# Feature maps of q for the last two batches: one projection and a crossbar transpose in place of a second projection

## The chip, the cores and the metric

The kernel runs on one core of one Trainium2 chip. The metric is the device time of one launch in microseconds. The core has TensorE (PE, with its weight loads PEld), VectorE (DVE), ScalarE (ACT), GpSimd (POOL, which here issues the loads) and SyncE (SP, which here issues transposes and stores).

## The reference

Linear attention with a softmax-like feature map, then a two-layer FFN with a squared ReLU. Eight batches of eight heads, 576 tokens, 64 columns a head; 128 features; the FFN goes from 512 over 2048 to 512.

```python
def phi(x):
    proj = np.einsum('bhsd,df->bhsf', x, w_phi)
    proj = proj - np.max(np.abs(proj), axis=-1, keepdims=True)
    return np.concatenate([np.exp(proj), np.exp(-proj)], axis=-1)
q_p, k_p = phi(q), phi(k)
kv  = np.einsum('bhsf,bhsd->bhfd', k_p, v);  z = np.sum(k_p, axis=2)
num = np.einsum('bhsf,bhfd->bhsd', q_p, kv)
den = np.einsum('bhsf,bhf->bhs', q_p, z)[..., None] + 1e-06
x = (num / den).transpose(0, 2, 1, 3).reshape(B * S, H * D)
h = np.maximum(x @ w_in, 0.0);  out = (h * h) @ w_out
```

## The kernel before

The attention of a batch and the FFN of a chunk of 512 tokens are interleaved: nine FFN chunks, the first 512 tokens of each batch as chunks 0 to 7, and the remaining 64 of all batches as chunk 8. The kernel first writes down some 1731 steps (`plan.add`), each with an engine, what it reads and writes, and the PSUM banks that it opens and closes. Then `arrange` puts them into the order of the table ORDER, with the bank of each from BASES and the choice between two engines from STATES. Every engine runs its own steps in that order and waits for what a step reads from others, so the table alone decides what stands behind what on each queue.

Of a batch (`attention`), in order of the steps' names:

- `Xk`, `Xq`: SP transposes the loaded, token-major xk and xq by DMA (18 blocks of 128x128) into kT and qT; xk, xq, kT and qT have two buffers, used by even and odd batches.
- `Pk`, `Mk`, `Ekp`, `Ekn`: projection of k (L354), its maximum (L409) and two exponentials (L415), token-major. `em`, `V`, `KV`, `kvc`: v is scaled by the maxima (L442), then kv is summed on PE (L472, L477) and copied to SBUF as bf16.
- The q side goes in five chunks c, four of 128 tokens by eight heads in half batches, and a last one of 64 tokens. `Pq` projects q token-major (L354) and `Mq` takes the maximum on DVE (L514); its exponential `en` scales the output later. `Fq` projects the same q a second time, feature-major (L549, two matmuls of 512 columns, of 256 for c = 4), and `Eqp`, `Eqn` take the exponentials on ACT (L564) into qp and qn.
- `NA`, `SA`, `NB`, `rd`, `xo`: numerators with qp (L579), scaled by `en` on DVE (L591), numerators with qn added, the reciprocal of the denominator (L599) and the product (L603). `Xx`: SP transposes xo into xT or xS (L637), the input of the FFN.

The FFN has `F1` (L719, four matmuls of 512 columns), `relu` (L694 on ACT or L696 on DVE), `sq` (L703), `F2` (L784), the copy `ot` (L195, L197) and the store `st` (L803).

Of the kernel before, what the change touches and what calls it, by code (L numbers as in the profile page):

```python
# [7 lines left out]
F32 = mybir.dt.float32  # L8
# [3 lines left out]
ACT = mybir.ActivationFunctionType  # L12
# [12 lines left out]
def dve_cost(n):  # L25
    return n / 960 + 0.064, n / 960 + 0.150 + SEM
# [85 lines left out]
def kernel(  # L112
# [41 lines left out]
    def sb(name, shape, dt=BF16):  # L154
        return pool.tile([P, *shape], dt, name=name)

    def ring(name, n, shape, dt=BF16):
        return [sb(f"{name}{i}", shape, dt) for i in range(n)]
# [19 lines left out]
    qp, qn = ring("qp", NQP, [8 * P]), ring("qn", NQP, [8 * P])  # L178
# [4 lines left out]
    mkn = sb("mkn", [36], F32)  # L183
# [132 lines left out]
    def attention(b):  # L316
# [181 lines left out]

        def qmax_ops(c):
# [17 lines left out]
            add("DVE", dve_cost(2 * n * Fd), fn, r=[pj], w=[("mq", s2, c)], closes=pj, what="Mq")  # L517
# [13 lines left out]

        qfeat = {}
# [128 lines left out]
        else:  # L661
# [17 lines left out]
            kv_ops(3)  # L679
            for c in range(5):  # L680
                qmax_ops(c)
            for c in range(5):
                q_ops(c)
                out_ops(c)
# [320 lines left out]
```

## Time and profile before

| what | before |
|---|---|
| median of 3 runs | 355.43 us (354.84 to 355.82) |
| span of the profiled execution (its own time is not listed) | 353.0 us |
| mean granted TensorE clock | 1.000 |
| PE, DVE, ACT, POOL busy | 340.7, 276.1, 226.8, 96.6 us |
| feature-major projections (L549) | 80 matmuls, 14.9 us busy |
| DMA transposes kT and qT; xT and xS | 6 and 6; 28 and 7 |

Busy times are unions of overlapping instructions: PE's matmuls are pipelined, and one of 512 columns lasts 379 ns in the table of groups while the next starts after 216 or so. What PE is waited for or waits for is therefore read from the chain of waits and not from the busy share. Batch 6's q side lies between about 210 and 257 us of the profile, batch 7's between about 235 and 286; after 300 us only FFN work is left.

### The profile page before, as it was taken

The numbers are of one execution on the slowest core, as the hardware profiler recorded it, in microseconds if no ns is written. First come the engines' busy times: TensorE is split into PE (matmuls) and PEld (weight loads), VectorE is DVE, ScalarE is ACT, GpSimd is POOL, SyncE is SP. The second block draws the span as 40 slices with busy tenths as digits, with TensorE's granted clock in tenths as the row PEclk, the third lists the DMA queues.
The fourth block names the chain that finished last, engine by engine and source line by source line (L and its number), as shares of the span: only waits on it lengthen the run. The fifth ranks groups of instructions, "written<-read, shape, count | busy, mean of one in ns | idle before, by whom it ended". The sixth has DMA issues, their size and how long they took to land.

```text
span 353.0 us, 8396 instructions
## 1 busy us (share of the span) xinstructions
PE 340.7 (97%) x3367; PEld 192.2 (54%) x3400; DVE 276.1 (78%) x524; ACT 226.8 (64%) x428; POOL 96.6 (27%) x144
## 2 busy tenths in 40 slices
PE   8889999999999999999999999999999999999995
PEld 5679875544654554545445654455555544444452
DVE  4999998899979988989678888799988727736210
ACT  4999887499688875785678577869676211340301
POOL 8745350488429300297001820000000000000000
PEclk9999999999999999999999999999999999999999
DMA  9999999899989976899354995600211211010105
GB/s 102 177 200 202 196 107 155 134 142 175 182 169 150 155 141 155 160 111 158 79 129 84 120 187 111 146 20 21 53 40 53 47 51 48 30 59 2 59 3 176
DMA packets 96101, 39.59 MB, mean 112 GB/s; under 512 B 64576, under 2 KB 91584, under 8 KB 96064
## 3 DMA queue, kind: packets, MB, share of 16 engines
q0 software_dynamic: 45216, 18.36, 45.6%
q1 hardware_dynamic: 50528, 20.42, 26.5%
q8 instruction: 26, 0.43, 0.5%
q10 hardware_dynamic: 320, 0.30, 0.3%
q14 instruction: 11, 0.09, 0.1%
HBM read 36.77 MB, written 9.44 MB: 131 GB/s over the span
## 4 chain that ended last, share of the span: by engine, by line
PE 79%; DVE 8%; ACT 6%; DMA 3%; issue 2%; SPq 0%; POOL 0%; DVEq 0%; ACTq 0%; POOLq 0%
PE psum L784 30%; PE psum L719 28%; PE psum L579 5%; PE psum L354 4%; PE psum L472 3%; PE psum L730 3%; PE psum L549 2%; DVE va L442 2%; DMA xq<-in_q_dram 1%; DVE mq L514 1%; ACT kp L415 1%; ACT kn L415 1%; DMA out_dram<-ot 1%; DVE mk L388 1%; DVE h L703 1%
## 5 line engine op out<-in xcount | busy, mean ns | idle before, releaser
L784 PE MATMUL psum<-wout,h 128*128 128x512 bf16 x527 | 128.4, 379 | 3.2 <-issue 1.3
L719 PE MATMUL psum<-xT,win 128*128 128x512 bf16 x448 | 106.1, 379 | 0.1
L694 ACT ACTIVATE hr<-psum 128x512 bf16<-128x512 f32 x96 | 55.3, 596 | 46.3 <-PE psum L719 24.3
L784 PEld LDWEIGHTS <-h 128*128 128x128 bf16 x560 | 50.2, 98 | 55.2 <-issue 2.0
L719 PEld LDWEIGHTS <-win 128*128 128x128 bf16 x512 | 47.4, 97 | 53.7 <-issue 3.1
L703 DVE TENSOR_TENSOR h<-hr 128x512 bf16<-128x512 bf16 x143 | 55.9, 415 | 16.4 <-ACT hr L694 15.6
L564 ACT ACTIVATE qp<-psum 128x1024 bf16<-128x1024 f32 (+1 forms) x40 | 37.4, 940 | 21.9 <-PE psum L549 21.5
L514 DVE TENSOR_REDUCE mq<-psum 128x8 f32<-128x1024 f32 (+1 forms) x40 | 44.1, 1110 | 4.0 <-PE psum L354 3.2
L409 DVE TENSOR_REDUCE mk<-psum 128x8 f32<-128x1024 f32 (+1 forms) x35 | 38.1, 1110 | 3.1 <-PE psum L354 3.1
L415 ACT ACTIVATE kp<-psum 128x1024 bf16<-128x1024 f32 (+1 forms) x35 | 32.8, 937 | 11.6 <-DVE mk L409 8.9
L564 ACT ACTIVATE qn<-psum 128x1024 bf16<-128x1024 f32 (+1 forms) x40 | 37.4, 939 | 1.3 <-PE psum L579 1.0
L696 DVE TENSOR_SCALAR hr<-psum 128x512 bf16<-128x512 f32 x48 | 32.6, 686 | 6.5 <-PE psum L719 5.2
L253 POOL DMA_DIRECT2D xv<-in_v_dram x26 | 19.4, 763 | 51.3 <-DVE va L442 48.0
L415 ACT ACTIVATE kn<-psum 128x1024 bf16<-128x1024 f32 (+1 forms) x35 | 32.8, 936 | 0.0
L442 DVE TENSOR_TENSOR va<-xv,va 64x256 bf16<-64x256 bf16 (+2 forms) x68 | 30.4, 462 | 1.6 <-ACT va L434 0.8
L591 DVE TENSOR_TENSOR psum<-psum,en 128x520 f32<-128x520 f32 (+1 forms) x40 | 27.6, 699 | 3.9 <-PE psum L579 2.5
L603 DVE TENSOR_TENSOR xo<-psum,rden 128x512 bf16<-128x512 f32 (+1 forms) x40 | 27.3, 686 | 1.0 <-DVE rden L599 0.2
L197 ACT ACTIVATE ot<-psum 128x512 f32<-128x512 f32 x18 | 10.7, 595 | 27.1 <-PE psum L784 27.1
L195 DVE COPY ot<-psum 128x512 f32<-128x512 f32 x17 | 11.5, 684 | 15.2 <-PE psum L784 7.9
L253 POOL DMA_DIRECT2D xk<-in_k_dram x28 | 20.6, 743 | 8.4 <-ACT va L428 4.0
L472 PE MATMUL psum<-va,kp 128*128 128x65 bf16 x256 | 19.6, 193 | 0.8 <-DVE va L442 0.4
L472 PE MATMUL psum<-va,kn 128*128 128x65 bf16 x256 | 19.6, 193 | 0.0
(69 smaller groups left out, 403.4 us busy)
## 6 DMA issues: line engine op xcount, KB each, us to landing
out_dram<-ot SPq DMA_DIRECT2D x32, 256.0 KB, 2.7
xk<-in_k_dram POOLq DMA_DIRECT2D x26, 128.0 KB, 4.3
xq<-in_q_dram POOLq DMA_DIRECT2D x24, 128.0 KB, 5.5
xv<-in_v_dram POOLq DMA_DIRECT2D x24, 128.0 KB, 4.2
win<-in_moe_w_in_dram POOLq DMA_DIRECT2D x4, 512.0 KB, 11.3
wout<-in_moe_w_out_dram POOLq DMA_DIRECT2D x4, 512.0 KB, 11.7
xq<-in_q_dram POOLq DMA_DIRECT2D x4, 256.0 KB, 5.8
xv<-in_v_dram POOLq DMA_DIRECT2D x2, 512.0 KB, 9.3
```

The lines of the kernel that those rows point to most:

```text
L253: pin(nc.gpsimd.dma_start(out=x[:, a * 512 : z * 512].rearrange("p (h x) -> p h x", x=4 * D), in_=src[b][2 * a : 2 * z, 0:512, :].rearrang ...
L409: pin(nc.vector.tensor_reduce(out=mk_view(g), in_=ps2(pj)[:, :, : n * Fd].rearrange("p e (i f) -> p e i f", f=Fd), axis=AX.X, op=ALU.max, ...
L415: pin(nc.scalar.activation(out=dst[slot][:, :, :n, :].rearrange("p e i f -> p e (i f)"), in_=ps2(pj)[:, :, : n * Fd], func=ACT.Exp, scale= ...
L442: pin(engine().tensor_tensor(out=t[:, :, :D].rearrange("p m (x c) -> p m x c", c=2), in0=x.rearrange("p (m x c) -> p m x c", m=n, c=2), in ...
L472: pin(nc.tensor.matmul(out=o[:, sg, hi, :], lhsT=(kp, kn)[sg][kgroup[pr]][:, j % 2, 2 * hi + j // 2, :], rhs=va[s2][sg][:, 8 * pr + 4 * hi ...
L514: pin(nc.vector.tensor_reduce(out=mqb[:, c, :, :n], in_=ps2(pj)[:, :, : n * Fd].rearrange("p e (i f) -> p e i f", f=Fd), axis=AX.X, op=ALU ...
L564: pin(nc.scalar.activation(out=o, in_=i_, func=ACT.Exp, scale=sgn))
L694: pin(nc.scalar.activation(out=hr[sl], in_=ps1(g), func=ACT.Relu))
L696: pin(nc.vector.tensor_scalar(out=hr[sl], in0=ps1(g), scalar1=0.0, scalar2=None, op0=ALU.max))
L703: pin(engine().tensor_tensor(out=dst, in0=i_, in1=i_, op=ALU.mult))
L719: pin(nc.tensor.matmul(out=o, lhsT=win[mc // 4][:, kc, mc % 4 * P : (mc % 4 + 1) * P], rhs=x, start=(kc == 0), stop=(kc == KC - 1)))
L784: pin(nc.tensor.matmul(out=ps1(g), lhsT=h2[c % 2][mc // 4][:, mc % 4, tt * P : (tt + 1) * P], rhs=wout[mc // 4][:, mc % 4, :], start=(mc = ...
```

## The change

For batches 6 and 7 (`LATE = 6`) the second, feature-major projection `Fq` is gone. The two exponentials (`Eq`) read the token-major projection of `Pq` after the maximum, and write bf16 over the first 2048 columns of the batch's own xk (c = 0, 2, 4) or xq (c = 1, 3), whose transposes into kT and qT are by then done. One DMA transpose on SP (`Xf`, 16 blocks of 128x128; for c = 4 two of 4 blocks) turns both into the tile qf, of which qp and qn are now the two halves. Batches 0 to 5 are as before. The steps of batches 6 and 7 are also written down in another sequence, and ORDER, BASES and STATES are new from step 900 on (of 1731): the first 900 rows of ORDER are the same. An unused tile, mkn, is dropped.

```diff
-    qp, qn = ring("qp", NQP, [8 * P]), ring("qn", NQP, [8 * P])
+    LATE = 6
+    qf = ring("qf", NQP, [2, 8 * P])
+    qp, qn = [t[:, 0, :] for t in qf], [t[:, 1, :] for t in qf]
...
-            add("DVE", dve_cost(2 * n * Fd), fn, r=[pj], w=[("mq", s2, c)], closes=pj, what="Mq")
+            turned = b >= LATE
+            add("DVE", dve_cost(2 * n * Fd), fn, r=[pj], w=[("mq", s2, c)] + [pj] * turned, closes=None if turned else pj, what="Mq")
+            if turned:
+                slot = qslot[0] % NQP
+                qslot[0] += 1
+                qfeat[c] = slot
+                src, qx = (("xk", xk), ("xq", xq))[c % 2]
+                qe = qx[s2][:, : 16 * P].rearrange("p (u x) -> p u x", u=2)
+                held = of(src, b, (0, 1, 2, 3, "s"))
+                for u, sgn in enumerate((1.0, -1.0)):
+                    def fn(u=u, sgn=sgn):
...
+                        pin(nc.scalar.activation(out=o, in_=i_, func=ACT.Exp, scale=sgn))
+                    add("ACT", act_cost(2 * n * Fd), fn, r=[pj], w=[pj] + held, closes=pj if u else None, what="Eq")
+                def fn():
+                    if c == 4:
+                        for u in range(2):
+                            pin(nc.sync.dma_start_transpose(out=qf[slot][:, u, : 4 * P].rearrange("f (x p) -> f x p", p=P),
+                                                            in_=qe[:, u, : 4 * Fd]))
+                    else:
+                        pin(nc.sync.dma_start_transpose(out=qf[slot].rearrange("f u (x p) -> f (u x) p", p=P),
+                                                        in_=qx[s2][:, : 16 * P]))
+                add("SP", (2.5 if c < 4 else 2.0, 0), fn, r=held, w=[("qp", slot), ("qn", slot)],
+                    dma=(3.2 * n / 4, HW_IN, "x", "kq"), what="Xf")
...
-            for c in range(5):
-                qmax_ops(c)
-            for c in range(5):
-                q_ops(c)
+            if b < LATE:
+                for c in range(5):
+                    qmax_ops(c)
+            for c in range(5):
+                if b < LATE:
+                    q_ops(c)
+                else:
+                    qmax_ops(c)
                 out_ops(c)
...
 ORDER = [
...
-    897, 903, 864, 1166, 689, 895, 915, 690, 1160, 813, 898, 815, 691, 926, 1164, 937, 899, 920, 973, 911, 921, 916,
...
+    974, 686, 891, 1030, 830, 925, 1159, 687, 863, 1158, 919, 908, 1366, 688, 909, 897, 903, 813, 689, 833, 864, 898,
```

Two places show what moves. The first is SP's queue from batch 5's last xT transposes to batch 6's xT. Buffers that end in 0 before the last number belong to even batches (kT0, xk0 are batch 6's), kT1, qT1, xk1, xq1 are batch 7's; xT1x are batch 5's outputs, xT0x batch 6's. Before:

```order
L637 DMA_TRANSPOSE xT11_129<-xo3_119 128x4x128
L803 DMA out_0_dram<-ot2_146 128x512
L338 DMA_TRANSPOSE qT1_83<-xq1_77 128x18x128
L338 DMA_TRANSPOSE kT1_81<-xk1_75 128x18x128
L803 DMA out_0_dram<-ot0_144 128x512
L803 DMA out_0_dram<-ot1_145 128x512
L637 DMA_TRANSPOSE xS_130<-xo4_120 128x4x64
L803 DMA out_0_dram<-ot1_145 128x512
L637 DMA_TRANSPOSE xT00_126<-xo0_116 128x4x128
```

And now:

```order
L665 DMA_TRANSPOSE xT11_126<-xo3_116 128x4x128
L544 DMA_TRANSPOSE qf0_110<-xk0_74 128x16x128
L339 DMA_TRANSPOSE kT1_81<-xk1_75 128x18x128
L544 DMA_TRANSPOSE qf1_111<-xq0_76 128x16x128
L339 DMA_TRANSPOSE qT1_83<-xq1_77 128x18x128
L544 DMA_TRANSPOSE qf2_112<-xk0_74 128x16x128
L835 DMA out_0_dram<-ot2_142 128x512
L544 DMA_TRANSPOSE qf0_110<-xq0_76 128x16x128
L835 DMA out_0_dram<-ot0_140 128x512
L835 DMA out_0_dram<-ot1_141 128x512
L665 DMA_TRANSPOSE xS_127<-xo4_117 128x4x64
L541 DMA_TRANSPOSE qf1_111<-xk0_74 128x4x128 x2
```

Batch 7's kT and qT transposes now stand between batch 6's new ones, kT ahead of qT, and batch 6's xT transposes follow all five chunks' Xf.

The second is ScalarE at batch 6's chunks 2 and 3 (psum is the tile with all eight banks; kp, kn are features of k, hr is the ReLU, en the scale of the output, kv0 batch 6's kv in SBUF). Before:

```order
L564 ACTIVATE qp2_112<-psum_61 128x1024
L694 ACTIVATE hr3_135<-psum_61 128x512
L428 ACTIVATE va11_101<-mk1_103 64x4x2
L564 ACTIVATE qn2_115<-psum_61 128x1024
L415 ACTIVATE kp4_88<-psum_61 128x1024
```

And now:

```order
L536 ACTIVATE xk0_74<-psum_61 128x1024 x2
L726 ACTIVATE hr0_128<-psum_61 128x512
L416 ACTIVATE kp1_85<-psum_61 128x1024
L726 ACTIVATE hr1_129<-psum_61 128x512
L429 ACTIVATE va11_101<-mk1_103 64x4x2
L416 ACTIVATE kn1_92<-psum_61 128x1024
L198 ACTIVATE kv0_108<-psum_61 128x260
L551 ACTIVATE en0_106<-mq0_104 128x8 x2
L536 ACTIVATE xq0_76<-psum_61 128x1024 x2
```

The exponentials go to xk0 and xq0 and not to qp and qn; the pair of a chunk now stands together, and those of chunks 2 and 3 stand on either side of the copy of kv.

More of the change, by code (lines that the diff above doesn't have):

```diff
@@ L182 @@
     xS = sb("xS", [4, KC, P])
-    mkn = sb("mkn", [36], F32)
     hr = ring("hr", 4, [TCH])
@@ L497, in q_ts @@
             return [(8 * (c // 2) + 4 * (c % 2) + i) if pe_in else 8 * (c % 2) + 2 * i + c // 2 for i in range(4)]
+        qfeat = {}
         def qmax_ops(c):
@@ L516, in fn @@
                     axis=AX.X, op=ALU.max, apply_absolute_value=True))
-            add("DVE", dve_cost(2 * n * Fd), fn, r=[pj], w=[("mq", s2, c)], closes=pj, what="Mq")
+            turned = b >= LATE
[9 more added lines that the diff above has]
+                    def fn(u=u, sgn=sgn):
+                        i_, o = ps2(pj)[:, :, : n * Fd], qe[:, u, : 2 * n * Fd]
+                        if c == 4:
+                            o, i_ = o.rearrange("p (i e f) -> p e i f", e=2, f=Fd), i_.rearrange("p e (i f) -> p e i f", f=Fd)
+                        else:
+                            o = o.rearrange("p (e x) -> p e x", e=2)
+                        pin(nc.scalar.activation(out=o, in_=i_, func=ACT.Exp, scale=sgn))
+                    add("ACT", act_cost(2 * n * Fd), fn, r=[pj], w=[pj] + held, closes=pj if u else None, what="Eq")
+                def fn():
+                    if c == 4:
+                        for u in range(2):
[6 more added lines that the diff above has]
+                    dma=(3.2 * n / 4, HW_IN, "x", "kq"), what="Xf")
             if c < 4:
@@ L530, in qmax_ops @@
                     add("ACT", act_cost(4), fn, r=[("mq", s2, 4)], w=[("en", s2, 4, hi)], what="en")
-        qfeat = {}
         def q_ops(c):
@@ L679, in attention @@
             kv_ops(3)
+            if b < LATE:
+                for c in range(5):
+                    qmax_ops(c)
             for c in range(5):
-                qmax_ops(c)
-            for c in range(5):
-                q_ops(c)
+                if b < LATE:
+                    q_ops(c)
+                else:
+                    qmax_ops(c)
                 out_ops(c)
@@ L948 @@
     '7762205543351613247724322302602306674447442731320126074760270660422244446264622606176160063720462403'
-    '6376440226246040224115440556605777123504024764140002202442402462567677750767766755006425602422242222'
-    '6400041712301603166777067742404660026444202224400017210165317677737366646061634664004006640006224525'
-    '2454225454357220664133466404400220620232550535444304162615557154625737570741465213753727542242756523'
-    '160'
+    '6376440226246040224115440556605777123504024764140002202442402462567677750767766755006427602426402022'
+    '6460011710301233161405027646464047026442041640066012336621271333100324242622764620606000244534255652'
+    '565475024630220646066406212665674044502120147454417627322770667152715043716571435312722414750'
 )
@@ L955 @@
     '0000000000000000010100110100110100010010000010000010000000000000100000001000100010100111000000001000'
-    '0010000000001010000000100010000101010000100010010001001001111111000110010000001000110100100101000010'
-    '011000000101100101001001111100011100100101111010010100010000111111000100001'
+    '0010000000001010000000100010000101010100100010000010001000010101101100100001110000001000010000110100'
+    '001100001010100010110101101100000010001101010001100010101101111000001111110'
 )
```

162 rows, old and new, of the table ORDER are left out of this document.

## The prediction

> **What bounds the kernel now.** I read the page first, then busy time by stretches, then the chain of waits of the stretches that the change touches, then the DMA transposes by line. All durations are of one profiled execution with a span of 353.0 us. Its own time is not listed; the median of the runs shown is 355.43, so 2.4 us lie around the span, and I set every sum against the span and add them back.
>
> ```profile
> span 353.0 us, 8396 instructions
> PE 340.7 (97%) x3367; PEld 192.2 (54%) x3400; DVE 276.1 (78%) x524; ACT 226.8 (64%) x428; POOL 96.6 (27%) x144
> ```
> ```profile
> core 0: us, PE busy (x) PEld busy (x) DVE busy (x) ACT busy (x) POOL busy (x), PEclk, DMA share, GB/s
> 186.00:206.00 20.00, 19.84 (x205) 10.86 (x204) 17.28 (x38) 13.88 (x27) 10.89 (x16) 1.00 0.81 101
> 206.00:226.00 20.00, 19.68 (x170) 9.82 (x171) 14.98 (x23) 14.82 (x27) 0.00 (x0) 1.00 0.90 177
> 226.00:246.00 20.00, 19.73 (x216) 11.04 (x215) 19.52 (x38) 16.80 (x35) 0.00 (x0) 1.00 0.05 18
> 246.00:266.00 20.00, 19.73 (x203) 10.63 (x205) 17.61 (x30) 14.25 (x28) 0.00 (x0) 1.00 0.16 41
> 266.00:286.00 20.00, 19.89 (x179) 10.35 (x180) 15.05 (x35) 8.64 (x14) 0.00 (x0) 1.00 0.26 57
> ```
>
> PE is never idle for long: in these 100 us the rows leave 1.13 us of it (100 less 98.87). DVE is nearly full once, from 226 to 246, and DMA is 0.8 to 0.9 busy up to 226 and nearly empty after. The chain says where PE sets the pace:
>
> ```profile
> by line: PE psum L784 45.0%; PE psum L719 42.2%; PE psum L579 4.9%; PE psum L472 1.9%; PE psum L748 1.9%; PE psum L549 1.7%; PE psum L354 1.1%; ACT qn L564 1.0%; issue 0.7%; PE psum L477 0.5%
> ```
> ```profile
> by line: DVE h L703 15.7%; ACT hr L694 12.8%; DVE va L442 9.3%; ACT kn L415 8.7%; ACT kp L415 8.7%; DVE hr L696 8.4%; issue 6.8%; ACT qn L564 6.5%; ACT qp L564 5.7%; DVE xo L603 4.3%; DVE psum L591 3.8%; ACT va L428 3.5%; ACT en L521 1.9%;
> ```
>
> The first row is the chain from 244 to 343 us: all PE but for 1.7%. The second is the chain from 228 to 244: no PE at all among the large shares, but VectorE and then ScalarE. So a PE instruction taken away after 244 shortens the end in full; one taken away between 228 and 244 does nothing by itself.
>
> **What goes: ten second projections.** Each chunk of q is projected twice now, token-major for the maximum (L354) and feature-major for the exponentials (L549). For batches 6 and 7 the second goes. The chain has nine of these ten in seven rows (a pair of matmuls each, x4 is two chunks); the first fence is the chain, the second the tenth chunk in the timeline:
>
> ```profile
> 210.48 0.22 PE psum L549 x2
> 224.25 0.32 PE psum L549 x2
> 247.62 0.32 PE psum L549 x2
> 254.25 0.22 PE psum L549 x2
> 257.16 0.43 PE psum L549 x4
> 269.38 0.54 PE psum L549 x4
> 285.06 0.22 PE psum L549 x2
> ```
> ```profile
> 240.27 0.39 PE L549 MATMUL psum<-qT,wphi 64*128 64x512 bf16 x2
> ```
>
> After 244 they take 0.32 + 0.22 + 0.43 + 0.54 + 0.22 = 1.73 us, all on the chain: -1.73. The two before 228 lie on PE stretches of the chain: -0.54. The one at 240.27 lies in the VectorE and ScalarE stretch: 0. Together -2.27 us; if only what lies after 244 counts, -1.73.
>
> **What is swapped at no cost.** The exponentials stay two to a chunk and of the same shape, but read the token-major PSUM tile and write bf16 over the batch's spent xk or xq; the maximum is unchanged.
>
> ```profile
> L564 ACT ACTIVATE qp<-psum 128x1024 bf16<-128x1024 f32 x32 | 32.7, 1026 | 11.5 <-PE psum L549 11.2 <-PE psum L579 0.2
> L514 DVE TENSOR_REDUCE mq<-psum x10: 676/1215/1225, 211.5 to 254.7; 128x8 f32<-128x1024 f32 x8, 128x4 f32<-128x512 f32 x2
> ```
>
> ```profile
> 241.40 0.91 ACT qp L564
> ...
> 244.53 0.86 PE psum L784 x4
> ...
> 259.65 0.48 PE psum L472 x16
> 260.13 0.12 PE psum L477 x2
> ```
>
> (The last fence is the chain again: one exponential, four FFN matmuls, and the 16 + 2 matmuls of one KV group.) So ScalarE and VectorE get neither more nor less work. One wait is new: the exponentials now stand behind the maximum of the same tile, 1.2 us later than they could be; what hides it is PE's other work, counted below.
>
> **What comes: twelve DMA transposes on SP** (eight of 16 blocks, four of 4), between exponentials and numerator matmuls (L579 before). The like of them is there already:
>
> ```profile
> L338 SPq DMA_TRANSPOSE kT<-xk x1: 2695/2695/2695, 220.3 to 220.3; - x1
> ...
> DMA to landing us min/median/max: 4.6/4.7/4.8
> ```
> ```profile
> L637 SPq DMA_TRANSPOSE xT<-xo x4: 1191/1220/1443, 246.6 to 254.4; - x4
> ...
> DMA to landing us min/median/max: 2.3/2.3/2.6
> ```
>
> 18 blocks hold SP 2.7 us and land after 4.6 to 4.8 (217 to 225 us); 4 blocks 1.2 and 2.3. Between them, 16 blocks: SP 1.2 + 12 x (2.7 - 1.2)/14 = 2.5 us, landing 2.3 + 12 x (4.6 - 2.3)/14 = 4.3. A chunk's way from projection to numerator is then 0.3 (matmul end) + 1.2 (maximum) + 2 x 0.9 (each holds the chain for 0.91) + 4.3 = 7.6 us, where before the feature-major exponentials fed the numerators directly. In the changed order PE has, between projection and numerator of batch 6's chunk 2, nine groups of four FFN matmuls at 0.86, four KV groups at 0.6 and small ones, some 11.3 us; of chunk 3, 10.8; the other eight chunks have 12.9 to 29. So 3.2 us are left at the tightest: cost 0. Without that cover each transpose would cost up to 4.3.
>
> The VectorE page of the Trainium skill (VectorE: DVE Perf Modes, section The three transpose paths and its Rules for kernel authors) speaks against this part: it puts a 128x128 block at 1309 ns by the crossbar against 390 on TensorE, and says to use TensorE where PSUM will do. By it 16 blocks would take 21 us; the trace's 18 blocks in 4.6 us (0.26 each) decide, and the sum goes by them.
>
> **What waits on SP behind them.** The rows for the work ahead, a page row and one of the chain:
>
> ```profile
> L603 DVE TENSOR_TENSOR xo<-psum,rden 128x512 bf16<-128x512 f32 (+1 forms) x40 | 27.3, 686 | 1.0 <-DVE rden L599 0.2
> ```
> ```profile
> 233.23 0.34 DVE h L703
> ```
> SP's queue is in order, so what stands behind a new transpose waits too. Batch 7's kT stands right behind the first new one, which waits for batch 6's second exponential. From batch 6's chunk-0 projection: 0.3 + VectorE's backlog ahead of the maximum (two xo at 0.69, two squarings at 0.34: 2.1) + 1.2 + some 3.0 of ScalarE (three exponentials and a small one) + 2.5 on SP + 4.6 to land = 13.7 us, against 13.5 of PE work up to the matmuls that read kT: +0.2. The ends of this term are 0 (no backlog on VectorE) and +2.3 (twice that backlog).
>
> **The order.** After step 900 every queue is rearranged, POOL's loads as well. It can remove gaps or make them. From below, all of the idle time that the rows of 186 to 286 show (1.1) and the store wait here (the chain leaves PE at 169 and comes back at 180; PE is idle for 1.0 of the 30 us around it) would go: -2.1. From above, as much again: +2.1. Nothing in the rows favours a sign: 0.
>
> ```profile
> 156.00:186.00 30.00, 29.00 (x269) 14.87 (x270) 24.61 (x46) 19.94 (x38) 9.06 (x14) 1.00 0.85 129
> ```
> ```profile
> 169.11 0.70 DVE xo L603
> ...
> 171.53 3.99 DMA out_dram<-ot
> ...
> 180.46 2.32 PE psum L784 x10
> ```
>
> Sum: 353.0 - 2.27 + 0.2 + 0 = 350.9 of span, 353.4 with what lies around it.
>
> **Rivals.** (1) Slower: transposes under loads. When a transpose meets the loads, it takes much longer:
>
> ```profile
> L338 SPq DMA_TRANSPOSE kT<-xk x1: 4903/4903/4903, 111.1 to 111.1; - x1
> ...
> DMA to landing us min/median/max: 11.0/11.0/11.0
> ```
> ```profile
> L637 SPq DMA_TRANSPOSE xT<-xo x4: 1191/1406/2208, 203.9 to 213.6; - x4
> ...
> DMA to landing us min/median/max: 2.7/5.8/6.5
> ```
>
> Batch 6's new transposes fall about where DMA is 0.90 busy (206 to 226). From 3.2 us of extra landing on, chunk 2's numerators hold PE; at 11.0 - 4.6 = 6.4 extra it is 3.2 us, and SP's longer issue (4.9 for 2.7) pushes chunk 3's by 2.2 more: 353.4 + 5.4 = 358.8 at worst, about 357.0 with two thirds of it. Against it: the 217 to 225 us transposes landed in 4.8 as loads ended. The Trainium skill (DMA: Bandwidth & Descriptors, Issuing engines are not separate DMA queues) says that transfers of all queues interleave on the same 16 DMA engines; the 11.0 against 4.7 agrees.
> (2) No change: the 16 us in which VectorE and ScalarE carry the chain grow forward and back. VectorE is at 19.5 of 20 us there, and its work is untouched; if batches 6 and 7 run at its pace, only the 0.22 + 0.54 + 0.22 after 257 or so stay, less the 0.2: 354.6. It decides where VectorE's share reaches PE's over a whole batch; over 186 to 246 it is 51.8 of 60, which speaks against.
> (3) Much faster: the order also saves its 2.1: 351.3.
> (4) Blocks cost in proportion to the 4-block landing (2.3/4 = 0.58 each): 16 take 9.3, the way is 12.6 against 10.8 to 11.3, some 1.5 us late at each of two chunks: 356.4. The 18-block rows exclude it nearly; the page's figure above is the same rule, only steeper.
>
> **Numbers.** About 0.3% (1.1 us) is what a measurement of this kernel can tell from no change. Forecast (gain of 1.1 to 3 us) 0.40, rival 3 0.12, rival 2 0.25, rival 1 0.22, rival 4 0.01. Faster 0.52 (forecast and rival 3), same 0.26 (rivals 2 and 4), slower 0.22 (rival 1). The range runs from 351.0 (the forecast with all of the order's 2.1 and a little more) to 357.0, which leaves out the worst half of rival 1 and what lies under rival 3. The forecast alone: 352.4 to 354.4.
>
> **What would show it.** Right: no feature-major projection after batch 5, PE's span shorter by about 2 us with the chain still all PE after 244; new transposes landing in 4 to 5 us; no numerator matmul named as waiting for SP or a DMA. Rival 1: landings over 7.5 us on batch 6's transposes and PE idle before its numerators. Rival 2: DVE and ACT shares of the chain up after 200 by 2 us. Rival 3: PE's idle time from 160 to 286 under half of now. Wrong altogether if PE waits for batch 7's kT or for xT of batches 5 to 7, whose transposes now queue among the new ones.

## The result and the profile after

The changed kernel takes 352.85 us (352.54 to 353.61, 4 runs) where the kernel before takes 355.13 (354.79 to 355.82, 4 runs): a ratio of 0.9937 [0.9925, 0.9948], 2.2 us less. Its profiled execution took 352.66 us, of which 350.5 are the span, 2.5 less than before. The page's first rows, and then the busy time by stretches (length, then busy us and instructions of each engine, clock, DMA share, GB/s):

```profile
span 350.5 us, 8394 instructions
PE 338.9 (97%) x3344; PEld 192.5 (55%) x3380; DVE 273.2 (78%) x521; ACT 228.4 (65%) x431; POOL 96.8 (28%) x144
```

```profile
156.00:186.00 30.00, 29.20 (x285) 15.45 (x287) 25.94 (x50) 25.70 (x50) 11.70 (x18) 1.00 1.03 141
186.00:206.00 20.00, 19.89 (x217) 11.45 (x218) 17.37 (x38) 13.79 (x26) 8.37 (x13) 1.00 0.66 95
206.00:226.00 20.00, 19.89 (x168) 9.91 (x168) 17.59 (x29) 17.25 (x29) 0.46 (x1) 1.00 1.09 165
226.00:246.00 20.00, 19.64 (x232) 11.39 (x231) 18.68 (x38) 14.82 (x30) 0.00 (x0) 1.00 0.60 122
246.00:266.00 20.00, 19.79 (x194) 10.67 (x196) 15.20 (x26) 14.86 (x25) 0.00 (x0) 1.00 0.66 135
266.00:286.00 20.00, 19.90 (x154) 10.31 (x155) 12.93 (x29) 4.57 (x11) 0.00 (x0) 1.00 0.43 96
```

PE's busy time is 1.8 us less. From 156 to 286 it is idle for 1.69 us (the lengths less the second number) where it was for 2.13, but this difference decides nothing: two further profiles of the changed kernel, taken with the experiments below, give 1.70 and 0.94. Work of DVE and ACT has come forward: from 206 to 226 they have 17.59 and 17.25 where they had 14.98 and 14.82. DMA stays busy to the end of these stretches, 0.43 to 1.09, where before it was 0.05 to 0.26 from 226 on.

The chain of waits of the changed kernel, by line, from 213 to 228 us and from 244 to 341 us:

```profile
by line: DVE va L443 19.9%; issue 17.5%; DVE mk L410 11.9%; DVE h L735 10.0%; PE psum L751 9.8%; DVE mq L517 7.6%; PE psum L816 6.5%; DVE psum L619 4.6%; DVE ot L196 4.1%; DVE xo L631 4.0%; DVE hr L728 2.2%; DVE rden L627 1.3%; PE psum L355
```
```profile
by line: PE psum L816 47.8%; PE psum L751 42.9%; PE psum L607 3.1%; PE psum L780 2.2%; PE psum L473 2.1%; PE psum L355 1.1%; issue 0.6%; PE psum L478 0.5%
```

The stretch that VectorE sets has moved from 228 to 244 to about 215 to 227, and ScalarE has gone out of it (the two further profiles of this kernel agree); after 244 the chain is PE as before, now without a feature-major projection. The new transposes (SP's part, first and last start, then landing for all of them):

```profile
L544 SPq DMA_TRANSPOSE qf<-xk x4: 1807/2422/3770, 211.4 to 260.3; - x4
L544 SPq DMA_TRANSPOSE qf<-xq x4: 1317/1776/1843, 217.3 to 269.9; - x4
...
DMA to landing us min/median/max: 4.2/4.5/6.3
```

Sixteen blocks hold SP for 1.3 to 3.8 us and land 4.2 to 6.3 us after their issue. Between 200 and 290 us the profile has one wait of PE of 0.2 us or more, and none for a transpose:

```profile
PE psum L355 <- DVE xo L631: 0.2, 1, 0.2
```

### The profile page after: what moved, and what is told of

Its sections match the earlier page's. It is cut to its first block, busy times and chain, and to the rows that moved or that the text cites. A ratio compares the mean times of both kernels' runs of the same rounds, so it can differ in the third digit from the quotient of the medians.

```text
span 350.5 us, 8394 instructions
## 1 busy us (share of the span) xinstructions
PE 338.9 (97%) x3344; PEld 192.5 (55%) x3380; DVE 273.2 (78%) x521; ACT 228.4 (65%) x431; POOL 96.8 (28%) x144
## 4 chain that ended last, share of the span: by engine, by line
PE 78%; DVE 10%; ACT 7%; issue 3%; DMA 1%; DVEq 0%; ACTq 0%; POOLq 0%
PE psum L816 30%; PE psum L751 27%; PE psum L607 5%; PE psum L355 4%; PE psum L473 3%; PE psum L762 3%; DVE va L443 3%; ACT qf L592 2%; PE psum L577 2%; DVE mk L410 2%; DVE mq L517 2%; DVE h L735 2%; ACT kn L416 1%; PE psum L780 1%; DMA xk<-in_k_dram 1%
## 5 line engine op out<-in xcount | busy, mean ns | idle before, releaser
L816 PE MATMUL psum<-wout,h 128*128 128x512 bf16 x524 | 130.1, 379 | 2.2 <-issue 0.6
L751 PE MATMUL psum<-xT,win 128*128 128x512 bf16 x448 | 108.1, 379 | 0.3
L726 ACT ACTIVATE hr<-psum 128x512 bf16<-128x512 f32 x97 | 56.3, 596 | 68.8 <-PE psum L751 43.7
L592 ACT ACTIVATE qf<-psum 128x1024 bf16<-128x1024 f32 (+1 forms) x60 | 54.6, 942 | 10.7 <-PE psum L577 9.4
L728 DVE TENSOR_SCALAR hr<-psum 128x512 bf16<-128x512 f32 x47 | 31.8, 685 | 17.7 <-PE psum L751 16.1
L607 PEld LDWEIGHTS <-qf 128*128 128x128 bf16 x640 | 28.3, 97 | 13.3 <-issue 1.1
L607 PE MATMUL psum<-kv,qf 128*128 128x65 bf16 x640 | 31.0, 193 | 0.0
L274 POOL DMA_DIRECT2D xq<-in_q_dram x24 | 17.6, 736 | 7.4 <-ACT kp L416 3.9
```

The source lines that it names most:

```text
L592: pin(nc.scalar.activation(out=o, in_=i_, func=ACT.Exp, scale=sgn))
L607: pin(nc.tensor.matmul(out=o[:, u // 4, u % 4 * D1 : (u % 4 + 1) * D1], lhsT=(qp, qn)[sg][slot][:, u * m : u * m + P], rhs=kv_sb[s2][:, h ...
L726: pin(nc.scalar.activation(out=hr[sl], in_=ps1(g), func=ACT.Relu))
L728: pin(nc.vector.tensor_scalar(out=hr[sl], in0=ps1(g), scalar1=0.0, scalar2=None, op0=ALU.max))
L751: pin(nc.tensor.matmul(out=o, lhsT=win[mc // 4][:, kc, mc % 4 * P : (mc % 4 + 1) * P], rhs=x, start=(kc == 0), stop=(kc == KC - 1)))
L816: pin(nc.tensor.matmul(out=ps1(g), lhsT=h2[c % 2][mc // 4][:, mc % 4, tt * P : (tt + 1) * P], rhs=wout[mc // 4][:, mc % 4, :], start=(mc = ...
```

## The experiments

Each was timed in five rounds beside the kernel before on the same chip. "Feature-major pair" is the two matmuls of one chunk that the change removes.

**The missing matmuls put back.** Into the changed kernel, ahead of each token-major projection of batches 6 and 7, into the same PSUM banks, which the projection then overwrites:

```diff
+                if what == "Pq" and b in PAID:                  # PAID = (6, 7)
+                    for u in range(2):
+                        r = slice(64 * u, 64 * u + 64)
+                        step = ts[1] - ts[0]
+                        pin(nc.tensor.matmul(out=o[:, u, : n * P].rearrange("f (i x) -> f i x", x=P), lhsT=wphi2[r, :],
+                                             rhs=xt[r, ts[0] : ts[-1] + 1 : step, :], start=True, stop=True))
```

> The changed kernel with PE's work of the second projection given back and nothing else: ahead of each token-major projection of batches 6 and 7 the two feature-major matmuls run into the same PSUM banks, and the projection then overwrites them. 8 pairs of 0.216 us and 2 of 0.11 are 1.95 us. Theory (the gain is PE time, since PE sets the pace): 1.5 to 1.95 us slower than the changed kernel's 352.85, so 354.4 to 354.8. Rival (the gain comes from the new order of the queues, PE time was hidden): no change, 352.6 to 353.2.

Measured: 353.83 us (353.62 to 354.46), ratio 0.9970 [0.9958, 0.9982]. Against the changed kernel's 0.9937 that is 0.33% or 1.2 us, some 60% of what PE was given and below the 1.5 to 1.95 expected. By the two intervals such a difference is good to some 0.6 us either way. The same with `PAID = (6,)` and with `PAID = (7,)`:

> As the run before it, for batch 6 alone: 4 pairs of 0.216 and one of 0.11, 0.97 us. Chunk 2's pair (and perhaps chunk 3's) lies where VectorE carries the chain in the changed kernel (215 to 227 us). Theory: 0.5 to 0.8 us slower than the changed kernel, 353.4 to 353.7. If PE time counts everywhere alike: 0.97, 353.8. Rival (order): 352.85.

> For batch 7 alone, 0.97 us of PE work at 243 to 262 us, where the chain is nearly all PE. Theory: 0.9 to 1.0 us slower than the changed kernel, 353.8. Rival (order): 352.85.

Measured: batch 6 alone 352.98 us (352.78 to 353.38), 0.9942 [0.9929, 0.9955], so 0.2 us of its 0.97, within the noise of nothing and below the 0.5 to 0.8 expected; batch 7 alone 353.61 us (353.0 to 354.74, 9 runs), 0.9964 [0.9952, 0.9977], so about 0.95 of its 0.97, though its runs spread over 1.7 us. The chains from 213 to 228 us, batch 6 paid and then batch 7 paid, fit this (lines after the insertion are 7 higher: L758 and L823 are FFN matmuls, L450 the scaling of v):

```profile
by line: PE psum L758 46.0%; PE psum L823 31.3%; PE psum L362 8.5%; PE psum L480 6.4%; PE psum L357 3.6%; PE psum L614 3.3%; PE psum L485 1.5%; issue 0.4%
```
```profile
by line: DVE va L450 19.9%; issue 17.5%; PE psum L758 14.1%; DVE mk L417 12.0%; DVE h L742 10.0%; DVE mq L524 7.5%; DVE psum L626 4.6%; PE psum L823 4.3%; DVE ot L197 4.1%; DVE xo L638 4.0%; DVE hr L735 2.2%; DVE rden L634 1.3%
```

With batch 6's pairs put back the stretch is all PE; without them it is VectorE's again, as in the changed kernel. So of the 0.97 us taken from PE there, VectorE's work, the next longest, lets only about 0.2 through. Batch 7's pairs lie behind that stretch, where the chain is PE, and count in full as far as 0.6 us of noise can tell.

**The missing matmuls in the old order.** The kernel before, with the pairs of batches 6 and 7 cut to 8 columns and the exponentials reading one column for all (the features of these batches are not computed):

```diff
+                    if b >= 6:
+                        pin(nc.tensor.matmul(out=o[:, u, :8], lhsT=wphi2[r, :], rhs=qTb[64 * u : 64 * u + 64, ts[0], :8], start=True, stop=True))
+                        continue
...
+                    if b >= 6:
+                        i_ = ps2(pf)[:, :, 0:1].to_broadcast([P, 2, n * P])
```

> The kernel before, in its own order, with the feature-major projection of batches 6 and 7 cut to 8 of its 512 (256) columns; the exponentials read one of these columns over and over, at the same size, so the output of these batches is not computed. It is the removal of PE time alone: no transposes, no new order. Theory: most of 1.95 us comes, 1.3 to 1.9 us faster than before (355.1), so 353.2 to 353.8. Rival (order): no change, 355.1.

Measured: 354.08 us (353.72 to 355.73, 12 runs), 0.9978 [0.9968, 0.9987]: 0.8 us, where 1.3 to 1.9 were expected. (A cut pair still holds PE for some 0.04 us, the time from its start to that of the next matmul, where a whole one holds it for 0.22; so some 1.6 of the 1.95 us were taken away, by estimate.) The chain by line from 206 to 228 us, in the kernel before and then in this one, and from 244 to 260 in this one (L789, L724 are FFN matmuls, L584 numerators):

```profile
by line: PE psum L784 55.4%; PE psum L719 25.9%; PE psum L354 9.6%; PE psum L579 4.6%; PE psum L549 2.9%; issue 1.4%; DVE va L442 0.9%
```
```profile
by line: PE psum L789 27.5%; DVE mq L514 14.3%; PE psum L724 14.2%; DVE mk L409 9.9%; issue 7.1%; DVE va L442 4.9%; PE psum L584 4.5%; ACT hr L699 4.5%; ACT kn L415 4.1%; PE psum L354 4.1%; DVE hr L701 3.1%; ACT ot L197 2.2%; ACT va L434 2.
```
```profile
by line: PE psum L789 43.2%; PE psum L584 10.7%; DVE va L442 9.9%; DVE mq L514 9.1%; DVE mk L409 7.2%; ACT kp L415 6.4%; PE psum L354 4.4%; DVE ot L195 4.3%; issue 3.4%; ACT va L434 0.7%; PE psum L550 0.7%; DVEq L442 0.1%; DVEq L195 0.1%
```

With the pairs whole the first stretch is PE but for 2.3%, and from 244 on the chain is PE but for 1.7%, as the prediction shows it. With the pairs cut, VectorE and ScalarE carry more than a third of both stretches. So in the old order too other engines ran close behind PE, before 244 and behind it, and took over when its work was taken away. The four kernels make a table (ratio to the kernel before):

| | pairs present | pairs away |
|---|---|---|
| old order | 1 | 0.9978 [0.9968, 0.9987] |
| new order, with transposes | 0.9970 [0.9958, 0.9982] | 0.9937 [0.9925, 0.9948] |

Read along the rows, the pairs are worth 0.8 us in the old order and 1.2 in the new; read down, the new order is worth 1.1 us with the pairs present and 1.5 without. The pairs are worth 2.27 in neither order. The differences within each of these two comparisons, 0.4 us, are not clear of the noise. One limit: the pairs put back stand beside other matmuls of 64 rows, where the chain before had 0.22 us for a pair; some of those removed had 0.32. So up to some 0.3 us of the pairs' worth may stand in the order's share.

**The changed kernel again**, as the reference on the chip of the next three:

> The changed kernel as it is, once more, on the chip of the next three: it is what they are read against. Every theory expects 352.9 us, a ratio of 0.994 to the kernel before.

Measured: 352.92 us (352.6 to 352.99), 0.9935 [0.9922, 0.9948].

**The mechanism in the old order.** Order, bank numbers and engine choices of the kernel before; of each chunk of batches 6 and 7:

```diff
-  Pq Mq ... Fq ... Eqp ... Eqn ... numerators      (before)
+         ... Pq Mq ... Eq ... Eq Xf ... numerators (no Fq; Xf on SP right behind the second Eq)
```

> The change's mechanism (exponentials from the token-major projection, transposes, no feature-major projections for batches 6 and 7) under the order, banks and engine choices of the kernel before: the token-major projection and the maximum stand where the feature-major projection stood, the transpose right behind the second exponential. The way from projection to numerator is some 7.6 us (5.5 for the short tile). The work that TensorE has between the two, by the order, is about 30, 18.7, 9.2, 2.7, 4.4 us for the tiles of batch 6 and 7.0, 20, 7.6, 9.3, 1.0 us for those of batch 7. Theory (the transposes are free only because the new order puts at least 7.6 us of TensorE work behind each projection): stalls of about 4.9, 1.1, 0.6 and 4.5 us, up to 11 us in all less the 0.8 us of the missing projections: 357 to 364 us, with TensorE idle behind a transpose at the fourth tile of batch 6 and the last of batch 7. Rival (the order is beside the point, and the gain is TensorE's missing work): 353 to 354 us.

Measured: 381.64 us (379.35 to 381.75), 1.0723 [1.0698, 1.0747]: 26.5 us slower than before. The direction is the theory's; but it is 28.7 us above the changed kernel, where up to 11 were expected. The page's first rows, then some stretches of 4 us, then the first instruction of PE's timeline behind each of its three longest stalls (idle time before an instruction in brackets), then its waits for transposes (us, times, longest):

```profile
span 379.8 us, 8385 instructions
PE 346.9 (91%) x3347; PEld 193.8 (51%) x3380; DVE 277.3 (73%) x524; ACT 226.8 (60%) x428; POOL 96.6 (25%) x144
```
```profile
250.00:254.00 4.00, 3.27 (x35) 1.67 (x33) 3.71 (x5) 1.77 (x2) 0.00 (x0) 1.00 0.74 164
254.00:258.00 4.00, 0.00 (x0) 0.00 (x0) 0.09 (x1) 2.10 (x4) 0.00 (x0) 0.93 0.70 133
258.00:262.00 4.00, 3.30 (x22) 1.84 (x24) 1.57 (x4) 0.00 (x0) 0.00 (x0) 0.50 0.00 0
262.00:266.00 4.00, 4.00 (x28) 1.80 (x27) 1.99 (x4) 0.72 (x2) 0.00 (x0) 0.72 0.26 60
...
282.00:286.00 4.00, 4.00 (x30) 1.84 (x29) 1.78 (x5) 0.96 (x2) 0.00 (x0) 0.66 0.00 0
...
312.00:316.00 4.00, 4.00 (x12) 1.49 (x11) 0.00 (x0) 0.00 (x0) 0.00 (x0) 0.57 0.00 0
```
```profile
258.48 0.62 PE L607 MATMUL psum<-kv,qf 128*128 128x65 bf16 x8 [5.21 <-DMA qf<-xq]
...
280.86 0.42 PE L607 MATMUL psum<-kv,qf 128*128 128x65 bf16 x8 [2.37 <-DMA qf<-xk]
...
311.29 0.42 PE L607 MATMUL psum<-kv,qf 128*128 128x65 bf16 x8 [2.94 <-DMA qf<-xk]
```
```profile
PE psum L607 <- DMA qf<-xq: 6.8, 2, 5.2
PE psum L607 <- DMA qf<-xk: 5.3, 2, 2.9
```

The chain where the longest stall lies:

```profile
250.97 1.24 DVE mq L517
...
252.23 1.16 ACT xq L536 x2
...
254.20 4.24 DMA qf<-xq
...
258.48 0.62 PE psum L607 x8
```

This is the way that the prediction added up, maximum, exponentials, transpose, numerator, now bare on the chain: 250.97 to 258.48 is 7.5 us where the prediction had 7.6 with the matmul's end. PE stood for 5.21 us of it, and then ran at a clock of 0.50. Over the span PE's idle time (span less busy) is 32.9 us against 11.6 in the changed kernel, 21.3 more, and its busy time 8.0 us more, for the same matmuls: together the 29.3 us between the spans. The waits for transposes are 12.1 us of it (6.8 and 5.3), close to the 11 that the theory counted. What it left out is the rest: 9.2 us of idle time at other waits, as a late chunk delays the work that was to cover the next one (argued, not shown step by step), and the 8.0 us. The low clock makes up at most 6.8 us of these 8.0 (a mean of 0.982 over 379.8 us leaves out 0.018 of it). What makes up the remainder is not shown; the profile's busy time is a union of overlapping matmuls, and in the kernel of the old engine choices below it grows by 5.3 us at a clock of 0.998.

The three stalls of 5.21, 2.37 and 2.94 us were each followed by a clock of 0.50 to 0.66 over 4 us, and it was back at 1.00 within 8 us; in this kernel the stalls of up to 1.68 us left it at 1.00. The Trainium skill (TensorE: Matmul & The Clock Gate, The HAM clock gate) has the array's clock at half after an idle window of some 3.4 us, and at full again after a busy window. The 0.50 and the return agree; but two of the three stalls were shorter than 3.4 us, so here 2.37 us of standing was enough.

**More transposing.** In the changed kernel a second transpose, of 8 blocks, ahead of each one of 16, into a tile that nothing reads:

```diff
+    scrap = sb("scrap", [8 * P])
...
+                    if c < 4:
+                        pin(nc.sync.dma_start_transpose(out=scrap.rearrange("f (x p) -> f x p", p=P), in_=qx[s2][:, : 8 * P]))
```

> The changed kernel with an extra transpose of 8 blocks into a tile that nothing reads, on SyncE ahead of each of the eight transposes of 16 blocks. By the trace of the changed kernel SyncE is busy 1.8 to 2.8 us with 16 blocks, so 0.9 to 1.8 us more each time, and the real transpose lands that much later, 5.5 to 6.5 us after its exponentials where it landed in 4.5. Theory (the transposes lie under at least 3 us of spare TensorE work): 352.9 to 353.4 us. Rival (transposes cost in proportion to their blocks, or collide with the loads): 64 blocks more on 160, and each microsecond of delay shown, 354.5 to 358 us.

Measured: 352.49 us (352.36 to 355.02, 6 runs), 0.9939 [0.9917, 0.9960], no difference from the changed kernel's 0.9935. The extra transposes, and then the real ones of 16 blocks (L547 here), in this kernel:

```profile
L541 SPq DMA_TRANSPOSE scrap<-xk x4: 1232/1278/2440, 208.8 to 260.0; - x4
L541 SPq DMA_TRANSPOSE scrap<-xq x4: 1232/1252/1759, 217.6 to 265.7; - x4
...
DMA to landing us min/median/max: 3.2/3.4/6.3
```
```profile
L547 SPq DMA_TRANSPOSE qf<-xk x4: 1915/3030/3406, 211.3 to 261.3; - x4
L547 SPq DMA_TRANSPOSE qf<-xq x4: 1317/1702/2169, 218.9 to 269.7; - x4
...
DMA to landing us min/median/max: 4.3/5.2/6.1
```

The real ones land 5.2 us after their own issue instead of 4.5, and the extra ones hold SP for 1.2 to 2.4 us each. The delay is smaller than was meant, though: an extra transpose reads what the first exponential of the chunk writes, and starts while the second still runs. Issue by issue, three of the eight real ones land 1.6 to 2.9 us later than in the changed kernel's profile, the other five within 0.6. The time shows none of it, to within some 0.8 us. The rival that each microsecond of delay shows is out, and so is a price in proportion to the blocks (64 more; the twelve transposes move 144, not the 160 of the expectation), which the rival put at 1.6 us or more.

**Batch 7's k ahead.** In the changed kernel's order, one step moved on SP's queue:

```diff
-    Xf(batch 6, chunk 0)  ...  Xk(batch 7)
+    Xk(batch 7)  Xf(batch 6, chunk 0)  ...
```

> The changed kernel with one step moved on SyncE: the transpose of batch 7's first k tile ahead of the first transpose of features instead of behind it. By the prediction's term for this queue 0.2 us is won (352.7 us). By the changed kernel's trace, where k landed at 219.15 us and TensorE first read it at 220.55, nothing is won, and the first transpose of features is 2.8 us later than before, under about 3 us of spare work: 352.9 us, at most 353.4.

Measured: 352.49 us (352.19 to 352.68), 0.9924 [0.9912, 0.9936], where the changed kernel on that chip had 0.9935 [0.9922, 0.9948]. Once more, with the changed kernel beside it:

> The kernel with batch 7's first k transpose ahead of the first transpose of features, once more, beside the changed kernel on the same chip: the first time it stood at a ratio of 0.9924 [0.9912, 0.9936] where the changed kernel had 0.9935 [0.9922, 0.9948]. If the 0.4 us is real, 0.3 to 0.5 us under the changed kernel again; if TensorE does not wait for this transfer, as the changed kernel's trace says, no difference: within 0.2 us.

> The changed kernel as it is, on the chip of the other three, for reading them against: 352.9 us, a ratio of 0.9935 to the kernel before.

Measured: 352.33 us (352.14 to 352.56), 0.9930 [0.9916, 0.9943], and the changed kernel 352.48 us (352.31 to 353.62), 0.9941 [0.9928, 0.9954]. The medians are 0.43 and 0.15 us apart and the ratios 0.0011 each time, with intervals that overlap. Not by PE's wait for k, at least. The transpose of k on SP and PE's first matmuls on that tile, in the changed kernel:

```profile
L339 SPq DMA_TRANSPOSE kT<-xk x1: 2815/2815/2815, 214.4 to 214.4; - x1
...
DMA to landing us min/median/max: 4.8/4.9/5.1
```
```profile
220.55 0.29 PE L355 MATMUL psum<-wphi,kT 64*128 64x128 bf16 x4
```

and in this one:

```profile
L339 SPq DMA_TRANSPOSE kT<-xk x1: 4002/4002/4002, 208.9 to 208.9; - x1
```
```profile
220.59 0.29 PE L355 MATMUL psum<-wphi,kT 64*128 64x128 bf16 x4
```

PE's start is the same though the transfer was issued 5.5 us earlier. The two ratios are the lowest of the study; that this kernel beats the changed one is not settled, and no cause is shown. At its earlier place k's transpose also went slower: it held SP for 4.0 us and landed 7.6 us after its issue.

**The new order with the old engine choices.** Relus and the copies of kv and of the output may run on ScalarE or on VectorE; in 71 of these steps of batches 5 to 7 and after the two kernels chose differently. The changed kernel with all 71 as before, everything else as changed:

```diff
-STATES = (...)   # of the changed kernel
+STATES = (...)   # 71 entries set back
```

> The changed kernel's order with the engine choices of the kernel before: where a step may run on ScalarE or VectorE (relus, copies of kv, copies of the output), 71 steps of batches 5 to 7 and of the blocks after them chose differently in the two kernels, and all 71 are set back. Theory (the new order's gain of about 1.1 us lies in the sequence together with these choices, since ScalarE and VectorE are each 87 % busy between 206 and 226 us): 353.8 to 355.5 us. Rival (the sequence alone carries it): 352.7 to 353.1 us.

Measured: 368.0 us (367.88 to 369.21, 4 runs), 1.0380 [1.0364, 1.0395]: 15.5 us above the changed kernel, far above what both theories gave. The first stretch, and what PE waits for from 156 to 290 us (us, times, longest):

```profile
156.00:186.00 30.00, 25.32 (x248) 13.41 (x247) 24.58 (x45) 17.92 (x36) 11.71 (x18) 1.00 0.92 109
```
```profile
PE psum L751 <- ACT hr L726: 2.2, 3, 0.9
PE psum L473 <- DVE hr L728: 2.2, 2, 1.6
PE psum L751 <- DVE mq L517: 1.8, 1, 1.8
PE psum L816 <- DVE hr L728: 1.2, 2, 1.0
```

PE is busy for 25.32 of 30 us instead of 29.20. From 156 to 290 us its waits for relus (hr) are 7.3 of the 12.4 us that have a name; in the first stretch alone they are 0.8 of 4.6, and the longest is one of 1.8 us for a maximum. That a step comes late on one engine with the other's turn already in the order is the likely reason, argued and not followed step by step. Sequence and engine choices are one plan; half of it is worse than none. So what in the order saves the 1.1 to 1.5 us cannot be divided between them.

**One batch further.** In the changed kernel the pairs of batch 5 cut to 8 columns in the same way as above (`if b == 5`; its features are not computed):

> The changed kernel with the feature-major projections of batch 5 cut from 512 (or 256) columns to 8, the exponentials reading one column broadcast (the features of batch 5 are not computed): TensorE loses another 0.92 us, at 156 to 198 us, where by the chain of the changed kernel VectorE and ScalarE end part of the work. It bounds what carrying the change on to batch 5 could bring at best in this order. Theory (missing TensorE work counts only where TensorE is the chain, so as for batch 6 it is mostly hidden): 352.5 to 352.8 us. Rival (TensorE's work counts everywhere): 352.0 us.

Measured: 352.34 us (351.88 to 352.75), 0.9931 [0.9919, 0.9944], against 0.9941 on that chip: 0.14 us by the medians, 0.35 by the ratios, of the 0.92 taken from PE, and the intervals overlap. (The time is below the theory's 352.5 to 352.8 because the changed kernel itself stood at 352.48 there and not at 352.9; the rival's difference of 0.9 did not come.) Its chain from 156 to 206 us:

```profile
by line: PE psum L756 29.7%; PE psum L821 16.2%; ACT kn L416 7.5%; PE psum L612 6.5%; DVE mk L410 5.9%; DVE h L740 4.3%; DVE xo L636 4.0%; PE psum L473 3.9%; issue 3.7%; DVE mq L517 3.6%; PE psum L355 2.6%; ACT hr L731 2.2%; ACT kp L416 2.0
```

VectorE and ScalarE carry a share of it, and most of what PE lost is hidden under them. In this order, carrying the change to batch 5 could bring at most about that.

## Why the prediction came out right

The time forecast was 353.4 and 352.85 came, the sign and the size of the likeliest case; but two of its terms were wrong by about 1 us each, in opposite directions, and that they cancel is luck.

- **The ten pairs, -2.27: too large.** They were worth 1.2 us in the new order and 0.8 in the old. The prediction took each pair that lay on a PE piece of the chain before as gained in full. A chain tells which work ended last, not by how much. In the new order batch 6's pairs lie where VectorE's work is nearly as long, and only some 0.2 of their 0.97 us came (batch 7's: 0.95 of 0.97). In the old order VectorE and ScalarE took over a good part of the chain when the pairs were cut, from 244 to 260 us as well. So the rule that a PE instruction taken away after 244 shortens the end in full did not hold; the lower value that it gave, -1.73, was nearer, but above both measured ones too. The durations of the chain's pieces, 0.32 for some pairs, can also hold more than the 0.22 that a pair costs beside its like.
- **The order, 0: too small.** It gave 1.1 us with the pairs present and 1.5 without (up to some 0.3 of it may belong to the pairs), inside the bounds of 2.1 either way. Nothing in the profile before told the sign, and the sum needed it.
- **Batch 7's kT on SP, +0.2: not there.** k was issued at 214.4 us and landed at most 5.1 us later, at 219.5; its first read at 220.55 left 1 us to spare, and moving it ahead did not move that read.
- **The twelve transposes, 0: right, with its mechanism.** The eight of 16 blocks landed in 4.5 us in the median for a forecast of 4.3 and held SP for 1.8 and 2.4 in the median for 2.5; half as many blocks again cost nothing that could be measured; and without the cover the way showed itself bare, 7.5 us for 7.6. Of the price without cover, up to 4.3 us for each transpose, PE's named waits are 12.1 us in four stalls; the longest, 5.2, is above 4.3, as PE stood from 253.27 us on and SP issued the transpose at 254.20. The whole price of the old order, 28.7 us, was more than twice those waits.
- **The exponentials behind the maximum: right.** ScalarE's waits before the exponentials on xk (us, times) come to 5.6 us, and PE has no wait of 0.2 us or more for them:

```profile
L536 ACT ACTIVATE xk<-psum x12: 592/1018/1036, 208.3 to 268.4; 128x1024 bf16<-128x1024 f32 x8, 128x512 bf16<-128x512 f32 x4
...
  DMA qf<-xk: 2.8, 1
  DVE mq L517: 2.8, 2
```

  2.8 us in two waits for the maximum; the other 2.8 us are a wait that the prediction did not name, for the previous transpose out of the same tile to be done before it is written again.
- **Rival 1 (transposes under loads): did not happen.** DMA was as busy as feared, 1.09 from 206 to 226 us, and batch 6's transposes of 16 blocks, from 211 to 232 us, landed as ever:

```profile
DMA to landing us min/median/max: 4.3/4.6/5.2
```

  It was nearer than the total says: transposes issued some 2.5 us ahead of the first of these were slow, k's 18 blocks in the kernel with k ahead (7.6 us to land) and the first 8 extra blocks in the one with more transposing (6.3). What slowed them is not shown.
- **Rival 2 (VectorE carries it): half true.** It is what hides batch 6's pairs; but the stretch became shorter, not longer, and some of the work of both engines came forward (206 to 226 us in the rows above).
- **Rival 3 (the order saves its 2.1 too): half of it.** The order brought 1.1 to 1.5 us. Its sign, PE's idle time from 160 to 286 under half, can't be read: from 156 to 286 three profiles of the changed kernel give 1.69, 1.70 and 0.94 us against 2.13 before. **Rival 4** fell with the landings.

So the total was right by two errors that happen to cancel; of 2.2 us some 0.8 to 1.2 came from the pairs (in the new order nearly all of it from batch 7) and the rest from the order. What in the order saves it stays open: its sequence and its choices of engine could not be tried apart.

## What to carry to other kernels

Work taken off the bounding engine counts in full only where that engine stays the last: before adding up its pieces on the chain, look at how far behind the second engine runs in that stretch, and count little where it is nearly full (0.2 of 0.97 us here). A slower path such as a transpose by DMA is free while the order puts more work between its ends than it is long (here 7.5 us), and without that cover it can cost more than its waits: 28.7 us for 12.1 us of them here, part of it by a lower clock. An order and its choices of engine are one thing: putting back half of the plan cost 15.5 us, seven times what the whole change had won.

## What was not expected of the hardware

- After TensorE had stood for 5.21, 2.37 and 2.94 us its granted clock fell, to 0.50, 0.66 and 0.57 over 4 us each; after stalls of up to 1.68 us in the same kernel, and 1.79 in the one with the old engine choices, it stayed at 1.00. Its mean over the span was 0.982 in the profiled run and 0.982 to 0.991 in all five, and the two with 0.986 and 0.991 were the shortest (379.74 and 379.35 us, the others 381.6 to 381.8). In every other kernel of the study the mean was between 0.997 and 1.
- Sixteen blocks issued behind eight extra ones landed 5.2 us after their own issue in the median, 0.7 us later than without; the time for which the extra ones hold the queue comes before that.
- Two transposes issued at about 208.8 us landed after 7.6 us (18 blocks) and 6.3 us (8 blocks); 16 blocks issued at 211.4 us in the changed kernel landed after 4.7.
- The mean busy share of the DMA engines can be above 1 (1.09), and transposes landed in the usual time there.
